# Reading the moving operand of every fp32r product in pairs from two halves of a tile

## The chip, the cores and the metric

The kernel runs on one core of one Trainium2 chip. The metric is the device time of one execution in microseconds. Five engines work side by side: TensorE (PE, with its weight loads shown as PEld), VectorE (DVE), ScalarE (ACT), GpSimd (POOL) and SyncE (SP), which here only issues DMAs.

## The reference, cut to what matters

Three stages follow one another: a block retention (linear attention with a decay per head), a mixture of eight experts whose gate is normalised by eight Sinkhorn rounds, and a dense layer with a non-linearity.

```python
def _moe_ref(x, w_gate, w1, w2):          # x 1536 x 512, w1 8 x 512 x 1024, w2 8 x 1024 x 512
    ...
    for e in range(E):
        h = np.maximum(x @ w1[e], 0.0)
        ye = h @ w2[e]
        out += P[:, e:e + 1] * ye

def _moe2_ref(x, w_in, w_out):            # w_in 512 x 2048, w_out 2048 x 512
    h = x @ w_in
    g = h - np.tanh(h)
    return (g @ w_out).astype(np.float32)
```

## The kernel before, in words

Everything is laid out by hand in one program order; each engine runs its instructions in that order and waits on semaphores.

**Retention** (the first 60 us) works on 12 chunks of 128 tokens with plain fp32 matmuls: `scores` (L234) multiplies keys by queries, `states` (L256) makes the running state, `outputs` (L270, L275) the result. Between the first scores and the rest, eight matmuls into a tile `still` (L357) only keep TensorE busy; their result is read by nobody. They read a tile of zeros, `zr`, as fp32r, 496 columns wide: twice from column 0, twice from column 8, twice from column 8 with the weights from column 8 as well, and twice a single column repeated 496 times. At the very start eight matmuls into `warm` (L185) do the same with bf16 zeros.

**Expert stage**: 96 steps (`NS`). A step `s` takes one half of one expert's hidden width and 512 tokens. The first product runs as seven 256-column products (Strassen's scheme) in `product` (L579, L581, L582); the second, in `second` (L477, L478, L480), is two groups of 512-column matmuls for four token tiles. To keep accuracy every operand is split into a high and a low part, both fp32r, and each product is the sum of three matmuls: high x high, high x low, low x high. So a step has 7 products x 2 k-halves x 3 = 42 matmuls of 256 columns, and 2 groups x 4 tiles x 3 = 24 matmuls of 512 columns.

**Dense stage**: 48 steps, each with 4 x 3 = 12 first matmuls of 512 columns (L689 to L691) and 4 x 3 = 12 second matmuls of 512 columns through `second`.

A matmul's stationary operand is loaded ahead of it (PEld); the moving operand (`rhs`) streams through. Moving are: the parts of `x1` (tiles `xph`, `xpl`, `xsh`, `xsl`, 256 columns a matmul) in the expert stage's first product, `x2` (`x2h`, `x2l`, 512 columns) in the dense stage's first, and the second weights (`w2h`, `w2l`, 512 columns) in `second`. These tiles are written by `split` (L131, L132): ACT copies the source into the high part, rounding it, and DVE (or POOL, for the dense stage's weights) subtracts that from the source to give the low part. `w2_split`, `part` and `turn` call it for `w2`, `x1` and `x2`.

```python
    def split(hi, lo, src, eng=nc.vector):
        nc.scalar.activation(out=hi, in_=src, func=ACTF.Copy)
        eng.tensor_tensor(out=lo, in0=src, in1=hi.bitcast(F32), op=ALU.subtract)
```

## Time and profile before

| | |
|---|---|
| median of 3 runs | 1321.54 us (1321.48 to 1322.59) |
| the profiled execution: time, span | 1320.67 us, 1318.9 us |
| TensorE matmul busy | 1309.5 us, 99% of the span |
| weight loads busy | 1160.9 us, 88% |
| VectorE busy | 916.4 us, 69% |
| ScalarE busy | 528.4 us, 40% |
| GpSimd busy | 275.2 us, 21% |

The time holds 1.8 us outside the span. A matmul's busy time reaches from its start to its end, and one starts before the last has drained, so a busy share of 99% says that TensorE is never without work, not how fast it streams. The speed is read from the distance between the starts of matmuls that follow each other.

### The profile page before, as it was taken

What the parts mean: (1) busy time and instruction counts of PE and PEld (TensorE: products, weight loads), DVE (VectorE), ACT (ScalarE), POOL (GpSimd) and SP (SyncE); (2) the same over time, 40 slices, a digit from 0 to 9 for tenths busy, and PEclk for the clock granted to TensorE, in tenths of its full rate; (3) what the DMA queues carried; (4) which work ended last, traced back from release to release, by engine and by line L of the source; (5) the groups of instructions that cost most, each with busy time, mean ns of one, the idle gap of its engine ahead of it and who ended that gap; (6) DMA issues with size and microseconds to landing.
All of it is one profiled execution on the core that took longest, in us unless ns stands there. A gap on an engine that the chain in (4) does not pass through costs nothing.

```text
span 1318.9 us, 20923 instructions
## 1 busy us (share of the span) xinstructions
PE 1309.5 (99%) x8377; PEld 1160.9 (88%) x8377; DVE 916.4 (69%) x1708; ACT 528.4 (40%) x1029; POOL 275.2 (21%) x325
## 2 busy tenths in 40 slices
PE   8999999999999999999999999999999999999998
PEld 6889999999999999999999999999999888888887
DVE  7877566766767576757667675757653587788887
ACT  2543223332323232333233332323232578776764
POOL 6511011221213121212222130322210102020200
PEclk9999999999999999999999999999999999999999
DMA  8301021222222121212112132222210011011001
GB/s 322 128 33 33 33 73 31 63 89 66 71 68 69 57 80 57 69 61 74 63 64 87 43 105 60 69 68 64 66 33 33 32 33 33 32 33 33 33 33 64
DMA packets 35666, 84.21 MB, mean 64 GB/s; under 512 B 4208, under 2 KB 12400, under 8 KB 35568
## 3 DMA queue, kind: packets, MB, share of 16 engines
q1 hardware_dynamic: 35568, 82.87, 19.3%
q8 instruction: 65, 1.06, 0.3%
q14 instruction: 33, 0.27, 0.1%
HBM read 71.32 MB, written 11.53 MB: 63 GB/s over the span
## 4 chain that ended last, share of the span: by engine, by line
PE 97%; DVE 1%; DMA 1%; issue 0%; ACT 0%; SPq 0%; ACTq 0%; DVEq 0%
PE yp L480 17%; PE yp L477 16%; PE yp L478 16%; PE ha L579 7%; PE ha L582 7%; PE ha L581 7%; PE hb L579 5%; PE hb L581 5%; PE hb L582 5%; PE g L691 3%; PE g L689 3%; PE g L690 3%; DMA qkv<-in_qkv 1%; PE sc L234 1%; PE o L275 0%
## 5 line engine op out<-in xcount | busy, mean ns | idle before, releaser
L508 ACT ACTIVATE hhia<-ha 128x512 fp32r<-128x512 f32 x96 | 57.6, 600 | 469.7 <-PE ha L582 465.8
L579 PE MATMUL ha<-xsh,w1h 128*128 128x256 f32 x576 | 162.0, 281 | 1.7 <-ACT s L600 1.7
L456 POOL TENSOR_TENSOR c<-c,d 128x256 f32<-128x256 f32 x64 | 47.8, 747 | 547.0 <-DVE d L455 547.0
L582 PE MATMUL ha<-xsh,w1l 128*128 128x256 f32 x576 | 161.0, 280 | 0.0
L581 PE MATMUL ha<-xsl,w1h 128*128 128x256 f32 x576 | 160.6, 279 | 0.0
L478 PE MATMUL yp<-w2l,hhia 128*128 128x512 f32 x384 | 149.4, 389 | 0.0
L480 PE MATMUL yp<-w2h,hloa 128*128 128x512 f32 x384 | 149.3, 389 | 0.0
L477 PE MATMUL yp<-w2h,hhia 128*128 128x512 f32 x384 | 149.3, 389 | 0.0
L480 PE MATMUL yp<-w2h,hlob 128*128 128x512 f32 x380 | 148.6, 391 | 0.0
L478 PE MATMUL yp<-w2l,hhib 128*128 128x512 f32 x380 | 147.9, 389 | 0.0
L477 PE MATMUL yp<-w2h,hhib 128*128 128x512 f32 x380 | 147.8, 389 | 0.0
L617 DVE TENSOR_TENSOR ha<-ha,s 128x256 f32<-128x256 f32 x96 | 41.4, 432 | 141.6 <-PE ha L582 141.6
L628 DVE TENSOR_TENSOR hb<-hb,s 128x512 f32<-128x512 f32 x96 | 66.9, 697 | 89.4 <-PE hb L582 89.3
L495 DVE SCALAR_TENSOR_TENSOR yacc<-yp,prob,yacc 128x512 f32<-128x512 f32 x168 | 118.8, 746 | 9.0 <-PE yp L480 9.0
L579 PEld LDWEIGHTS ha<-xsh,w1h 128*128 128x128 f32 x576 | 108.2, 188 | 9.1 <-ACT s L600 1.9
L581 PEld LDWEIGHTS ha<-xsl,w1h 128*128 128x128 f32 x576 | 108.2, 188 | 7.4
L582 PEld LDWEIGHTS ha<-xsh,w1l 128*128 128x128 f32 x576 | 108.8, 189 | 0.0
L579 PE MATMUL hb<-xph,w1h 128*128 128x256 f32 x384 | 106.7, 278 | 0.0
L581 PE MATMUL hb<-xpl,w1h 128*128 128x256 f32 x384 | 106.3, 277 | 0.0
L582 PE MATMUL hb<-xph,w1l 128*128 128x256 f32 x384 | 106.1, 276 | 0.0
L480 PEld LDWEIGHTS yp<-w2h,hloa 128*128 128x128 f32 x384 | 72.1, 188 | 15.0
L480 PEld LDWEIGHTS yp<-w2h,hlob 128*128 128x128 f32 x380 | 71.3, 188 | 14.9
(160 smaller groups left out, 3330.6 us busy)
## 6 DMA issues: line engine op xcount, KB each, us to landing
wraw<-in_w SPq DMA_DIRECT2D x64, 512.0 KB, 4.8
d<-in_wio SPq DMA_DIRECT2D x64, 256.0 KB, 2.9
qkv<-in_qkv SPq DMA_DIRECT2D x23, 512.0 KB, 6.9
wscr<-c SPq DMA_DIRECT2D x64, 128.0 KB, 1.8
wraw<-wscr SPq DMA_DIRECT2D x16, 512.0 KB, 4.4
out<-yacc SPq DMA_DIRECT2D x12, 256.0 KB, 2.1
qkv<-in_qkv SPq DMA_DIRECT2D x2, 256.0 KB, 4.5
lamb<-in_lam SPq DMA_DIRECT2D x1, 4.0 KB, 2.5
```

The source lines that it names most:

```text
L456: nc.gpsimd.tensor_tensor(out=c1.bitcast(F32), in0=c1.bitcast(F32), in1=lo.bitcast(F32), op=ALU.mult)
L477: nc.tensor.matmul(out=yp, lhsT=a[:, ts], rhs=w2h[q][:, i], start=first, stop=False)
L478: nc.tensor.matmul(out=yp, lhsT=a[:, ts], rhs=w2l[q][:, i], start=False, stop=False)
L480: nc.tensor.matmul(out=yp, lhsT=c[:, ts], rhs=w2h[q][:, i], start=False, stop=last)
L495: nc.vector.scalar_tensor_tensor(out=y, in0=yp[t], scalar=prob[:, b * TPB + t, u // 2:u // 2 + 1], in1=y, op0=ALU.mult, op1=ALU.add)
L508: nc.scalar.activation(out=a, in_=ps, func=ACTF.Relu)
L579: nc.tensor.matmul(out=ps, lhsT=w1h[q][:, ws], rhs=xh[:, k], start=start and k == 0, stop=False, skip_group_check=True)
L581: nc.tensor.matmul(out=ps, lhsT=w1h[q][:, ws], rhs=xl[:, k], start=False, stop=False, skip_group_check=True)
L582: nc.tensor.matmul(out=ps, lhsT=w1l[q][:, ws], rhs=xh[:, k], start=False, stop=k == 1, skip_group_check=True)
L617: nc.vector.tensor_tensor(out=pa[:, hi], in0=pa[:, lo], in1=s5, op=ALU.add)
L628: nc.vector.tensor_tensor(out=pb, in0=pb, in1=s12, op=ALU.add)
L689: nc.tensor.matmul(out=ph, lhsT=w1h[q][:, ws], rhs=x2[b][0][:, k], start=k == 0, stop=False)
```

## The change

The moving tiles are stored in another column order, and read back in the old one. `halves` views a stored row as two halves, `odds` views a source row as its even columns and then its odd ones; a split therefore writes the even columns into the first half and the odd ones into the second. `pairs` reads a stored row as column 0 of the first half, column 0 of the second, column 1 of the first, and so on, which is the original order. Results, their order in PSUM, weights and the number of fp32r products stay as they are. The two halves lie 128 columns (512 bytes) apart in `x1`, and 256 columns (1024 bytes) apart in `x2` and the second weights. The sources of the splits are now read with a step of two columns. Beside that the eight fp32r matmuls of `still` become eight bf16 ones of 512 columns.

```diff
+    def halves(a):
+        return a.rearrange("p (t n) -> p t n", t=2)
+    def odds(a):
+        return a.rearrange("p (n t) -> p t n", t=2)
+    def pairs(a):
+        return a.rearrange("p (t n) -> p n t", t=2)
...
-        split(w2h[q][:, i], w2l[q][:, i], wraw[q][:, 1024 + 512 * i:1536 + 512 * i],
+        split(halves(w2h[q][:, i]), halves(w2l[q][:, i]), odds(wraw[q][:, 1024 + 512 * i:1536 + 512 * i]),
...
-        cols = slice(128 * (c % 2), 128 * (c % 2) + 128)
-        hi, lo = (x1[c // TPB][kind, j][:, i:i + n].rearrange("p c (k m) -> p (c k) m", k=2)[:, :, cols]
+        cols = slice(64 * (c % 2), 64 * (c % 2) + 64)
+        hi, lo = (x1[c // TPB][kind, j][:, i:i + n].rearrange("p c (k t m) -> p (c k) t m", k=2, t=2)[:, :, :, cols]
                   for j in range(2))
-        split(hi, lo, src)
+        split(hi, lo, src.rearrange("p k (m t) -> p k t m", t=2))
...
-    for w, rhs in ((0, zr[:, 0:496]), (0, zr[:, 8:504]), (8, zr[:, 8:504]), (0, zr[:, 0:1].to_broadcast([128, 496]))):
-        for i in range(2):
-            nc.tensor.matmul(out=still[:, 0:496], lhsT=zr[:, w:w + 128], rhs=rhs, start=True, stop=True)
+    for i in range(8):
+        nc.tensor.matmul(out=still, lhsT=zero[:, 0:128], rhs=zero, start=True, stop=True)
...
-                        nc.tensor.matmul(out=yp, lhsT=a[:, ts], rhs=w2h[q][:, i], start=first, stop=False)
-                        nc.tensor.matmul(out=yp, lhsT=a[:, ts], rhs=w2l[q][:, i], start=False, stop=False)
+                        nc.tensor.matmul(out=yp, lhsT=a[:, ts], rhs=pairs(w2h[q][:, i]), start=first, stop=False)
+                        nc.tensor.matmul(out=yp, lhsT=a[:, ts], rhs=pairs(w2l[q][:, i]), start=False, stop=False)
...
-        split(x2[b][0][:, k], x2[b][1][:, k], ps)
+        split(halves(x2[b][0][:, k]), halves(x2[b][1][:, k]), odds(ps))
...
-            nc.tensor.matmul(out=ps, lhsT=w1h[q][:, ws], rhs=xh[:, k], start=start and k == 0, stop=False,
+            nc.tensor.matmul(out=ps, lhsT=w1h[q][:, ws], rhs=pairs(xh[:, k]), start=start and k == 0, stop=False,
                              skip_group_check=True)
...
-                nc.tensor.matmul(out=ph, lhsT=w1h[q][:, ws], rhs=x2[b][0][:, k], start=k == 0, stop=False)
+                nc.tensor.matmul(out=ph, lhsT=w1h[q][:, ws], rhs=pairs(x2[b][0][:, k]), start=k == 0, stop=False)
```

No instruction of the products changes its place on TensorE; the one place in that engine's order that differs is `still`, in the first 10 us between the first chunk's scores (`sc`) and its state (`stp`). Before:

```order
L234 MATMUL sc_0_174<-qkv_122 128x128
L234 MATMUL sc_1_175<-qkv_122 128x128
L357 MATMUL still<-zr 128x496 x8
L256 MATMUL stp_204<-qkv_122 64x64 x8
L275 MATMUL o_213<-at_184,qkv_122 64x128 x8
```

After the change, at the same place (the lines of the file have moved by 8 or 9):

```order
L243 MATMUL sc_1_175<-qkv_122 128x128
L365 LDWEIGHTS zr
L365 MATMUL still<-zr 128x512
...
L365 LDWEIGHTS zr
L365 MATMUL still<-zr 128x512
L265 MATMUL stp_204<-qkv_122 64x64 x8
L284 MATMUL o_213<-at_184,qkv_122 64x128 x8
```

Eight matmuls stay eight; they are bf16 and 512 columns wide now. On ScalarE the splits of the first block's `x1` (`xph`, `xsh`, from the retention results `xr` and their sums `ts`) before the change:

```order
L289 ACTIVATE xr_283<-o_271 128x512
L131 ACTIVATE xph_89<-xr_225 128x4x128
L289 ACTIVATE xr_338<-o_318 128x512
L131 ACTIVATE xph_89<-xr_283 128x4x128
L289 ACTIVATE xr_390<-o_370 128x512
L131 ACTIVATE xph_89<-xr_338 128x2x128
```

and after it:

```order
L298 ACTIVATE xr_283<-o_271 128x512
L140 ACTIVATE xph_89<-xr_225 128x8x64
L298 ACTIVATE xr_338<-o_318 128x512
L140 ACTIVATE xph_89<-xr_283 128x8x64
L298 ACTIVATE xr_390<-o_370 128x512
L140 ACTIVATE xph_89<-xr_338 128x4x64
```

The instructions and their order are the same; each writes twice as many runs of half the length.

## Rows read from the trace of the kernel before

**Rows 1.** Page, part 1: busy time, share of the span, instructions of each engine.

```profile
PE 1309.5 (99%) x8377; PEld 1160.9 (88%) x8377; DVE 916.4 (69%) x1708; ACT 528.4 (40%) x1029; POOL 275.2 (21%) x325
```

**Rows 2.** Waits of TensorE, whole span: total us, times, longest.

```profile
PE sc L234 <- DMA qkv<-in_qkv: 2.1, 2, 1.3
PE ha L579 <- ACT s L600: 1.7, 1, 1.7
PE warm L185 <- DVE bias L186: 1.5, 1, 1.5
```

**Rows 3.** Stretches: busy us (count) of PE, PEld, DVE, ACT, POOL; granted clock; DMA.

```profile
60.00:1058.00 998.00, 996.27 (x6390) 903.48 (x6387) 659.44 (x1303) 325.81 (x671) 201.96 (x256) 1.00 0.19 60
10.00:60.00 50.00, 48.80 (x812) 41.86 (x807) 41.19 (x71) 19.53 (x39) 36.41 (x33) 1.00 0.69 247
...
1100.00:1200.00 100.00, 100.00 (x440) 82.39 (x439) 80.53 (x121) 72.97 (x129) 16.99 (x13) 1.00 0.13 43
```

**Rows 4.** Timeline of TensorE, 400 to 410 us: start, duration, line, operation.

```profile
400.66 0.39 PE L477 MATMUL yp<-w2h,hhib 128*128 128x512 f32 x1
...
402.93 0.39 PE L478 MATMUL yp<-w2l,hhib 128*128 128x512 f32 x1
...
403.39 0.28 PE L579 MATMUL ha<-xsh,w1h 128*128 128x256 f32 x1
...
404.09 0.28 PE L579 MATMUL hb<-xph,w1h 128*128 128x256 f32 x1
...
404.44 0.28 PE L579 MATMUL hb<-xph,w1h 128*128 128x256 f32 x1
...
405.57 0.28 PE L581 MATMUL hb<-xpl,w1h 128*128 128x256 f32 x1
```

**Rows 5.** Timeline of TensorE, single matmuls of `still` between 7.7 and 9.3 us.

```profile
7.76 0.39 PE L357 MATMUL still<-zr 128*128 128x496 f32 x1
...
8.66 0.39 PE L357 MATMUL still<-zr 128*128 128x496 f32 x1
8.89 0.37 PE L357 MATMUL still<-zr 128*128 128x496 f32 x1
9.10 0.37 PE L357 MATMUL still<-zr 128*128 128x496 f32 x1
```

**Rows 6.** Tile `still` by itself: duration in ns, lowest, median, highest; starts.

```profile
L357 PE MATMUL still<-zr x8: 372/386/492, 7.4 to 9.1; 128*128 128x496 f32 x8
```

**Rows 7.** Timeline of the weight loads in the retention stage.

```profile
22.43 0.64 PEld L234 LDWEIGHTS sc<-qkv 64*128 64x128 f32 x10
```

**Rows 8.** Line L234 by itself: duration in ns, lowest, median, highest.

```profile
L234 PEld LDWEIGHTS sc<-qkv x192: 182/188/188, 6.3 to 49.9; 64*128 64x128 f32 x192
```

**Rows 9.** Groups of instructions by line and form: the splits.

```profile
L131 ACT ACTIVATE w2h<-wraw 128x512 fp32r<-128x512 f32 x80 | 46.7, 624 | 0.0
L132 DVE TENSOR_TENSOR w2l<-wraw,w2h 128x512 fp32r<-128x512 f32 x64 | 45.0, 704 | 26.7 <-ACT w2h L131 26.7
L131 ACT ACTIVATE w1h<-wraw 128x256 fp32r<-128x256 f32 x32 | 13.0, 407 | 0.0
```

**Rows 10.** The same view: operations that read unit steps, or steps of two and eight.

```profile
L460 DVE SCALAR_TENSOR_TENSOR c<-d,c 128x256 f32<-128x256 f32 x64 | 35.7, 558 | 7.3 <-DVE d L459 0.5
L451 DVE SCALAR_TENSOR_TENSOR c<-c,c 128x256 int32<-128x256 int32 x64 | 27.2, 425 | 2.2
L456 POOL TENSOR_TENSOR c<-c,d 128x256 f32<-128x256 f32 x64 | 47.8, 747 | 547.0 <-DVE d L455 547.0
L457 POOL TENSOR_TENSOR c<-c,c 128x256 f32<-128x256 f32 x64 | 47.3, 740 | 5.0
L418 DVE TENSOR_REDUCE cs<-csum 128x8 f32<-128x96 f32 x8 | 2.0, 255 | 9.0 <-PE csum L415 9.0
L402 DVE TENSOR_REDUCE mx<-logits 128x1 f32<-128x96 f32 x1 | 0.2, 246 | 0.0
```

**Rows 11.** Timeline of the start: the eight opening matmuls on bf16 zeros.

```profile
1.45 3.60 PE L185 MATMUL warm<-zr 128*128 128x512 bf16 x8 [1.45 <-DVE bias L186]
```

## The prediction

> **What bounds the kernel now.** I read the page first: TensorE is busy 99% of the span and no other engine more than 69% [rows 1]. Busy on TensorE does not mean streaming at full speed, so two questions follow: does it wait for anyone, and how fast does it go while it doesn't? The waits answer the first: the longest of all are 2.1 us for a load and 1.7 us for ScalarE [rows 2]. [...] So the kernel is as long as the matmuls that follow each other.

> The timeline answers the second. Between the first and the last 512-column row there are ten starts in 2.27 us, 227 ns a matmul; between the last two 256-column rows ten starts in 1.13 us, 113 ns; in the stretch before them (the product that reads `xsh`) six starts in 0.70 us, 117 ns [rows 4]. The 100 us of the dense stage hold 440 matmuls, 227 ns each [rows 3]. [...]

> [...] Of the eight matmuls of `still`, those that read 496 columns one after the other start 226 ns apart (five starts from 7.76 to 8.89 us), whether reading and weights begin at column 0 or 8; the one that repeats a single column needs 0.21 us until the next starts [rows 5], and the shortest of the eight, 372 ns, is 14 ns below their median of 386 [rows 6]. Same type, same loads of weights, same zeros: only where the moving columns lie differs. [...] The change keeps all columns and reads them from two places in turn; the trace has no matmul of 256 or 512 columns that reads that way, and the sum rests on how much of the broadcast's speed it gets.

> **The change, part by part.**

> *The 512-column matmuls.* Per expert step 24, per dense step 24: 96 x 24 + 48 x 24 = 3456. [...] I take 216 ns, between the two and near the broadcast, the one row in which the loss answered to where the columns lie: 3456 x 11 ns = **38.0 us**.

> *The 256-column matmuls.* 96 x 42 = 4032. Here a second limit lies close: each needs a load of 128 weight columns. In the retention stage's scores the loads, two row halves side by side, come in pairs: ten loads in 0.64 us, the last of which takes 0.188 us, so 0.452 us for four steps, 111 to 113 ns a step [rows 7, 8], although each step there streams no more than 2 x 128 columns. I take 112 ns as the closest that such loads come. From 113.4 ns (227 halved) that gives 4032 x 1.4 ns = **5.6 us**. Bounds: nothing, if the loads set the 113 ns already; 4032 x (115.5 - 109) = 26 us, if the broadcast's speed holds here and the 117 ns go too (115.5 is the middle of 113.4 and 117 weighted by the timeline's steps: a step's 24 x 227 + 42 x 113.4 ns is 10.21 us, while 998 us by 96 steps is 10.40).

> *The splits.* Their number and order stay; the sources are read with a step of two columns. POOL shows no price for that: 747 ns where one input has a step of two, 740 without [rows 10]. DVE shows at most 558 - 425 = 133 ns for 256 columns [rows 10] (different operations, so some of it may be theirs), 266 ns on a low part of 512 columns that takes 704 [rows 9]. ACT has no such row: between nothing and a doubled time by the column, 2 x (624 - 407) = 434 ns on 624 [rows 9]. In three expert steps (31 us) two second weights are split: 0.5 us on DVE, 0.9 us on ACT, beside idle times of 10 and 21 us [rows 3]. A second weight is split about three steps ahead of its use, so nothing is late. In the retention stage DVE is busy 41 of 50 us [rows 3] and the `x1` splits lie near the path; 10,500 columns of low parts, from there to step 3, at 0.52 ns are 5.5 us against 9 us of idle time. I take nothing, with 3 us as the upper bound.

> *`still`.* Eight matmuls for eight. At 210 ns by the broadcast they save 0.1 us; if they stream as slowly as the eight opening ones, 3.60 / 8 = 0.45 us each [rows 11], they cost 1.8 us. I take nothing.

> **Sum.** 38.0 + 5.6 = 43.6 us. The profiled execution took 1320.67 us, so 1277.1; the median is 0.9 us higher, so **1278 us**. Once TensorE is 3.4% faster, DVE's 81% in the dense stage (5% shorter then, since all its matmuls have 512 columns) becomes 85%: still no bound.

> [...]

> [...]

> [...]

> [...]

> [...]

> **How the numbers follow.** Faster, by all or a good part of the sum: 0.52. If half of the loss stays on the 512 columns, 3456 x 5.5 + 5.6 = 25 us are left, less 3 us of splits 1300 us; if both matmuls reach their lower bounds, 3456 x 14 + 26 is 74 us, of which I allow 65, since both at once are unlikely. So this case's own range is 1256 to 1300. No change: 0.12. A little slower, up to 1396: 0.16. Half rate: 0.20, the one case that the range leaves out. Range: 1256 to 1396. What a measurement can tell from no change is about 0.2%, 2.6 us; so faster 0.52, same 0.12, slower 0.36.

> **What would show it.** In the timeline of the changed kernel, ten 512-column starts in 2.16 us (2.27: no change; 2.4 and more: the slower ways), ten 256-column starts in 1.12 us; in the dense stage's 100 us some 463 matmuls for 440. The waits of TensorE should stay under 10 us in all; low parts of second weights between 704 and 970 ns on DVE. I am wrong if the spacing doesn't move, if it grows, or if 256 columns go below 112 ns, which would say that loads are not their limit.

## The result, and the profile after

The changed kernel takes 1280.88 us (median of 4 runs, 1279.1 to 1281.2), the kernel before 1321.99 us in the same runs: a ratio of 0.9686 (95% interval 0.9669 to 0.9703), 41 us less. 1278 us was forecast. The profiled execution took 1280.69 us with a span of 1278.9.

The page's first part, and the waits of TensorE over the whole span (total us, times, longest), to be held against [rows 1, 2]:

```profile
PE 1264.7 (99%) x8377; PEld 1154.7 (90%) x8377; DVE 927.2 (72%) x1708; ACT 546.1 (43%) x1029; POOL 276.8 (22%) x325
```

```profile
PE ha L587 <- ACT s L608: 2.7, 3, 2.1
PE yp L485 <- ACT ghi L665: 1.6, 2, 0.8
PE sc L243 <- DMA qkv<-in_qkv: 1.5, 2, 1.3
PE yp L485 <- DVE yacc L501: 1.5, 2, 0.8
```

TensorE is as busy by share as before, and waits a little more: the second and fourth rows are new and lie in the dense stage (a third new one, 0.8 us for the gate's logits, lies in the retention stage). DVE and ACT are busy 11 and 18 us longer with the same instructions. The gain is in the distance of the matmuls. The timeline of TensorE, for [rows 4]:

```profile
401.90 0.38 PE L485 MATMUL yp<-w2h,hhib 128*128 128x512 f32 x1
...
404.06 0.38 PE L486 MATMUL yp<-w2l,hhib 128*128 128x512 f32 x1
...
404.49 0.27 PE L587 MATMUL ha<-xsh,w1h 128*128 128x256 f32 x1
...
405.16 0.28 PE L587 MATMUL hb<-xph,w1h 128*128 128x256 f32 x1
...
406.28 0.28 PE L589 MATMUL ha<-xpl,w1h 128*128 128x256 f32 x1
```

Ten 512-column starts take 2.16 us, 216 ns each (227 before). The six starts of the product that reads `xsh` take 0.67 us, 112 ns each (117 before), ten of the others 1.12 us, 112 ns (113 before).

The same holds over the whole trace. I call a distance between two starts a stop where it is over 160 ns at 256 columns or over 260 ns at 512. Without the stops, the 3455 recorded distances at 512 columns average 227.3 ns before and 216.0 after, the 4032 at 256 columns 114.9 and 111.6: 39.1 and 13.6 us gained. What the stops take beyond these averages grows from 4.3 to 15.2 us. There are 77 stops after the change, and the rows of `ha` and `yp` above count seven waits: most stops are too short to leave TensorE idle.

The splits of the second weights, for [rows 9] (busy us, mean ns):

```profile
L140 ACT ACTIVATE w2h<-wraw 128x512 fp32r<-128x512 f32 x80 | 66.0, 868 | 0.0
...
L141 DVE TENSOR_TENSOR w2l<-wraw,w2h 128x512 fp32r<-128x512 f32 x64 | 53.8, 841 | 25.4 <-ACT w2h L140 25.4
```

868 ns for 624 on ACT, 841 for 704 on DVE. One thing more happened at the start of the expert stage: stretches of the profile (the last columns are granted clock, DMA share, GB/s).

```profile
68.20:71.00 2.80, 2.80 (x8) 2.26 (x7) 2.06 (x4) 2.80 (x5) 0.00 (x0) 0.50 0.00 0
72.00:78.00 6.00, 6.00 (x44) 5.68 (x44) 5.43 (x10) 1.47 (x4) 0.00 (x0) 1.00 0.31 92
```

TensorE had waited 2.1 us for ACT shortly before (the longest wait above); then it ran at a granted clock of 0.50 for some 3 us, in which its 512-column matmuls start 427 ns apart. That costs 8 x 211 ns = 1.7 us. The profile of before has a wait of 1.7 us there and no such fall. The length of the wait doesn't decide it, though: the run with the storage alone (below) has 1.8 us and the fall (a granted clock of 0.94 from 50 to 80 us, as in the changed kernel), and the first set of reading orders, which is the changed kernel up to its end, has 2.1 us and no fall (1.00 over its span). What decides it stays open.

### The profile page after: what moved, and what is told of

Its sections match the earlier page's. It is cut to its first block, busy times and chain, and to the rows that moved or that the text cites. A ratio compares the mean times of both kernels' runs of the same rounds, so it can differ in the third digit from the quotient of the medians.

```text
span 1278.9 us, 20923 instructions
## 1 busy us (share of the span) xinstructions
PE 1264.7 (99%) x8377; PEld 1154.7 (90%) x8377; DVE 927.2 (72%) x1708; ACT 546.1 (43%) x1029; POOL 276.8 (22%) x325
## 4 chain that ended last, share of the span: by engine, by line
PE 79%; DVE 13%; ACT 4%; POOL 1%; DMA 1%; issue 1%; SPq 0%; ACTq 0%; POOLq 0%; DVEq 0%
PE yp L485 13%; PE yp L488 13%; PE yp L486 13%; PE ha L587 7%; PE ha L590 6%; PE ha L589 6%; PE hb L587 5%; PE hb L590 5%; PE hb L589 5%; DVE tb L688 2%; DVE yacc L501 2%; DVE tb L687 2%; DVE ta L680 2%; DVE g L685 1%; DVE ta L683 1%; PE g L697 1%
## 5 line engine op out<-in xcount | busy, mean ns | idle before, releaser
L485 PE MATMUL yp<-w2h,hhia 128*128 128x512 f32 x384 | 146.7, 382 | 0.0
L488 PE MATMUL yp<-w2h,hloa 128*128 128x512 f32 x384 | 146.3, 381 | 0.0
L486 PE MATMUL yp<-w2l,hhia 128*128 128x512 f32 x384 | 146.3, 381 | 0.0
L485 PE MATMUL yp<-w2h,hhib 128*128 128x512 f32 x380 | 144.4, 380 | 0.0
L488 PE MATMUL yp<-w2h,hlob 128*128 128x512 f32 x380 | 144.1, 379 | 0.0
L486 PE MATMUL yp<-w2l,hhib 128*128 128x512 f32 x380 | 144.1, 379 | 0.0
```

Of the source, the lines that this page charges most:

```text
L485: nc.tensor.matmul(out=yp, lhsT=a[:, ts], rhs=pairs(w2h[q][:, i]), start=first, stop=False)
L486: nc.tensor.matmul(out=yp, lhsT=a[:, ts], rhs=pairs(w2l[q][:, i]), start=False, stop=False)
L488: nc.tensor.matmul(out=yp, lhsT=c[:, ts], rhs=pairs(w2h[q][:, i]), start=False, stop=last)
```

## The experiments

In each of the runs compared by time the kernel before was timed beside it (1322.2 to 1323.6 us).

**The reads alone.** The tiles stored in natural order, still read in pairs; the columns or tokens come out in another order.

```diff
-        split(halves(w2h[q][:, i]), halves(w2l[q][:, i]), odds(wraw[q][:, 1024 + 512 * i:1536 + 512 * i]),
+        split(w2h[q][:, i], w2l[q][:, i], wraw[q][:, 1024 + 512 * i:1536 + 512 * i],
...
-        split(halves(x2[b][0][:, k]), halves(x2[b][1][:, k]), odds(ps))
+        split(x2[b][0][:, k], x2[b][1][:, k], ps)
```

> Reading in pairs stays, but the tiles are stored in their natural order again, so all outputs come with columns or tokens in another order; the splits read and write as before the change. Theory (the gain is the order in which TensorE reads, the price is the split with a step of two): 512 columns 216 ns, 256 columns 112 ns apart, ACT's copy of a second weight back from 868 to 624 ns, and the waits of TensorE in the dense stage (four of 0.9 us, several of 0.1 us) mostly gone: 1274 to 1277 us. Rival 1 (those waits come from the shorter step, not from the splits): 216 and 112 ns, 1281 us. Rival 2 (the gain comes from the storage or from other engines' timing and not from the reads): 227 and 113 ns, 1321 us.

1276.36 us, ratio 0.9653 (0.9641 to 0.9666), ACT's copy at 621 ns. So the whole gain comes with the order of reading, and rival 2 falls. The change is 4.5 us slower than this run, but not all of that is shown to be the price of its splits. Of 5.4 us between the two profiled spans (1278.9 and 1273.5), 1.7 us are the lower clock, which this run didn't have (1.00 from 50 to 80 us); 1.5 us lie before the first `ha` starts (56.3 and 54.8 us), and there the two sets of reading orders below, with the change's own instructions, have 54.5 and 58.8; 1.8 us are stops in the expert stage (7.8 and 6.0), 0.5 us the dense stage. The waits in the dense stage didn't go: `yp` still waits 1.8 us for high parts and 0.8 for `yacc`, and 0.7 to 0.9 us are missing between two starts in four places. Rival 1 holds for these.

**The storage alone.** Splits as in the change, all reads one column after the other.

```diff
-                        nc.tensor.matmul(out=yp, lhsT=a[:, ts], rhs=pairs(w2h[q][:, i]), start=first, stop=False)
+                        nc.tensor.matmul(out=yp, lhsT=a[:, ts], rhs=w2h[q][:, i], start=first, stop=False)
```

(and so for each `pairs`.)

> The tiles are stored with even columns first, but read one column after the other, so outputs come in another order. Theory: 227 and 113 to 117 ns as before the change, the slower splits hidden behind TensorE: 1321 to 1323 us. Rival 1 (the splits' price lies on the path whatever TensorE's speed): 1327 us. Rival 2 (storage makes the gain): 1281 us.

1323.12 us, ratio 1.0003 (0.9991 to 1.0014): nothing is gained or lost by storage. Its row for the same copy holds a surprise:

```profile
L140 ACT ACTIVATE w2h<-wraw 128x512 fp32r<-128x512 f32 x80 | 49.5, 658 | 0.0
```

The same instruction, with the same step of two, takes 658 ns here and 868 in the changed kernel. With TensorE reading one column after the other the step costs 34 ns (658 for 624 before the change); the other 210 appear in the changed kernel, in which TensorE reads in pairs.

**512 columns alone.** `x1` stored and read as before the change, the second weights and `x2` as after it.

> Only the second weights and x2 (512 columns a matmul) are stored and read in pairs; x1 is stored and read as before the change. Theory (256 columns gain 1.6 ns at 113 and 5 ns at 117, because the weight loads hold them at 112): the 512-column matmuls keep all of their gain, 256 columns go back to 113 and 117 ns, which costs 4032 x 2.4 = 10 us: 1290 us. Rival (the 256-column matmuls are bound by weight loads before the change as well, and gain nothing): 1281 us.

1286.99 us, ratio 0.9733 (0.9721 to 0.9746). The 512-column matmuls bring 35 us of the gain, the 256-column ones 6.1 us more (1286.99 - 1280.88; 5.6 forecast, 10 in the expectation). That is their net worth: by the traces their distance falls from 114.6 ns here to 111.6 in the change, 12 us, of which the change loses 2.9 us again in stops of the expert stage (4.9 here, 7.8 there) and 1.7 us at the lower clock.

**What order costs what.** Groups of eight matmuls behind the kernel's end, each on its own line, for instance

```diff
+    for i in range(8):
+        nc.tensor.matmul(**look(w[:, 0:512], 512, 128))
+    for i in range(8):
+        nc.tensor.matmul(**look(w[:, 0:512].rearrange('p (t n) -> p n t', t=2), 512, 128))
```

with `w` the 1024 columns of a second weight, then the columns and the number of weight columns.

> The changed kernel with 33 groups of eight matmuls behind its end, on second weights of the last step, each group with another order of reading; their results are not used. Spacing in a group tells the price of the order. Theory (a new stretch of 16 columns costs one column's time if the reader stands in one stretch only, and two open stretches hide it): one after the other 227 ns at any offset; halves in pairs, and quarters in fours, 216; runs of 2, 4 and 8 columns from each half 216, runs of 16 and 32 back at 227; pairs at a distance of 2 to 8 columns 227, from 16 on 216; one column repeated 213 to 216, 16 columns over and over 216, 32 columns over and over 227; step 2, with twice as many new stretches, 240; step 16, each column a new stretch, 430 or more. Rival (the loss depends on which part of the memory neighbouring reads fall in, not on stretches): pairs differ by distance beyond 16 too, and quarters differ from halves. At 256 columns, theory (weight loads hold 112 ns): one after the other 113, pairs 112, one column repeated 112, pairs with 64 weight columns 109, 192 columns 112 in either order, 128 columns 112. Rival (the streaming holds 112): repeated 109, pairs with 64 weight columns 112, 192 columns 85.

The timeline of TensorE there, at a granted clock of 1.00 and with all other engines idle; the distance in a group is its start to the next row's, divided by eight.

```profile
1273.66 1.98 PE L723 MATMUL mb<-w2h,w2l 128*128 128x512 f32 x8
1275.48 1.89 PE L725 MATMUL mb<-w2h,w2l 128*128 128x512 f32 x8
1277.20 2.03 PE L727 MATMUL mb<-w2h,w2l 128*128 128x512 f32 x8
1279.08 2.43 PE L729 MATMUL mb<-w2h,w2l 128*128 128x512 f32 x8
1281.34 3.77 PE L731 MATMUL mb<-w2h,w2l 128*128 128x512 f32 x8
1284.93 3.86 PE L733 MATMUL mb<-w2h,w2l 128*128 128x512 f32 x8
1288.61 3.65 PE L735 MATMUL mb<-w2h,w2l 128*128 128x512 f32 x8
1292.08 2.84 PE L737 MATMUL mb<-w2h,w2l 128*128 128x512 f32 x8
1294.75 2.17 PE L739 MATMUL mb<-w2h,w2l 128*128 128x512 f32 x8
1296.76 2.11 PE L741 MATMUL mb<-w2h,w2l 128*128 128x512 f32 x8
1298.71 2.08 PE L743 MATMUL mb<-w2h,w2l 128*128 128x512 f32 x8
1300.63 2.06 PE L745 MATMUL mb<-w2h,w2l 128*128 128x512 f32 x8
1302.52 2.01 PE L747 MATMUL mb<-w2h,w2l 128*128 128x512 f32 x8
1304.37 1.89 PE L749 MATMUL mb<-w2h,w2l 128*128 128x512 f32 x8
1306.09 1.89 PE L751 MATMUL mb<-w2h,w2l 128*128 128x512 f32 x8
...
1314.73 1.89 PE L761 MATMUL mb<-w2h,w2l 128*128 128x512 f32 x8
1316.45 2.09 PE L763 MATMUL mb<-w2h,w2l 128*128 128x512 f32 x8
1318.38 2.06 PE L765 MATMUL mb<-w2h,w2l 128*128 128x512 f32 x8
1320.28 1.91 PE L767 MATMUL mb<-w2h,w2l 128*128 128x512 f32 x8
1322.03 2.02 PE L769 MATMUL mb<-w2h,w2l 128*128 128x512 f32 x8
1323.88 1.11 PE L771 MATMUL mb<-w2h,w2l 128*128 128x256 f32 x8
1324.83 1.06 PE L773 MATMUL mb<-w2h,w2l 128*128 128x256 f32 x8
1325.72 1.06 PE L775 MATMUL mb<-w2h,w2l 128*128 128x256 f32 x8
1326.62 1.10 PE L777 MATMUL mb<-w2h,w2l 128*64 128x256 f32 x8
1327.56 1.04 PE L779 MATMUL mb<-w2h,w2l 128*64 128x256 f32 x8
1328.44 1.04 PE L781 MATMUL mb<-w2h,w2l 128*128 128x192 f32 x8
1329.31 1.05 PE L783 MATMUL mb<-w2h,w2l 128*128 128x192 f32 x8
```

| 512 columns read | line | ns |
|---|---|---|
| one after the other, from column 0, the same again, from column 8 | 723, 769, 727 | 228, 231, 235 |
| halves in pairs | 725 | 215 |
| quarters in fours | 729 | 283 |
| step 2, 4, 16 | 731, 733, 735 | 449, 460, 434 |
| two from each half in turn | 737 | 334 |
| 4, 8, 16, 32 from each half in turn | 739, 741, 743, 745 | 251, 244, 240, 236 |
| pairs 2, 4 columns apart | 747, 749 | 231, 215 |
| pairs 8, 16, 32, 64, 128 columns apart | 751 to 759 | 216 on average |
| each column twice | 761 | 215 |
| 16, 32 columns over and over | 763, 765 | 241, 238 |
| one column repeated | 767 | 219 |

My theory of new stretches of 16 columns falls: the same 16 columns over and over (241 ns) are as slow as new ones (228 to 235), two, four or eight from each half (334, 251, 244) are slower than one after the other, and quarters (283) are not fast. Its rival has the quarters right, but not the pairs, which from 4 columns' distance on are all alike (215 and 216). A step of two takes 449 ns, twice the 228 of one after the other: the half rate that I feared for pairs.

At 256 columns the theory holds: one column repeated (L775) 112 ns, pairs (L773) 111, pairs with 64 weight columns (L779) 110, and 192 columns one after the other (L781) still 109 although at 227 ns for 512 they would stream in 85 ns. So something other than the columns holds these matmuls at 109 to 112 ns. That it is the load of 128 weight columns fits the 111 to 113 ns in the prediction and the 110 with 64 weight columns, but no group had fewer columns and fewer weights at once. One after the other from `w` (L771) they take 119.

```diff
+        nc.tensor.matmul(**look(w[:, 0:512].rearrange('p (b t n) -> p b n t', t=2, n=4), 512, 128))
...
+        nc.tensor.matmul(**look(w[:, 2:514].rearrange('p (b t n) -> p b n t', t=2, n=4), 512, 128))
...
+        nc.tensor.matmul(**look(w.rearrange('p (t n s) -> p n t s', t=2, s=2)[:, :, :, 0], 512, 128))
```

> Behind the end of the changed kernel, again groups of eight matmuls with other orders of reading; their results are not used. The first set said: one after the other 227 to 239, pairs from 4 columns' distance on 216, runs of two from each half 333, 16 columns over and over 240. Theory formed from it (the reader takes even and odd places of the stream separately, each keeps one line of 4 columns, 16 bytes, and loses time when it leaves a line after fewer than four reads of its own): halves in pairs from column 2 on 216; pairs at 4 columns' distance from column 2 on (each side leaves its line after two reads) 227 to 240, at 8 columns' distance from column 2 on between 216 and 230; halves 255 columns apart 215 for 510 columns; halves 512 columns apart 216; pairs whose halves are read at a step of two (two reads a line and side) 227 to 240; at a step of four (one read a line), 256 columns, 180 or more; each column four times 216; every second column twice (two reads a line and side) 227 to 240; every fourth column twice (one read) 350 or more. Rival (a pair is fast as soon as its two columns lie in different lines, since one after the other both want the same line at once): pairs at 4 and 8 columns' distance from column 2 on 216, halves at a step of two 216, halves at a step of four 108 to 112; every second column twice 227, like one after the other.

The timeline of TensorE in the second set:

```profile
1281.54 1.89 PE L727 MATMUL mb<-w2h,w2l 128*128 128x512 f32 x8
1283.27 1.89 PE L729 MATMUL mb<-w2h,w2l 128*128 128x512 f32 x8
1285.00 1.99 PE L731 MATMUL mb<-w2h,w2l 128*128 128x512 f32 x8
1286.83 1.98 PE L733 MATMUL mb<-w2h,w2l 128*128 128x512 f32 x8
1288.64 1.89 PE L735 MATMUL mb<-w2h,w2l 128*128 128x510 f32 x8
...
1292.09 2.02 PE L739 MATMUL mb<-w2h,w2l 128*128 128x512 f32 x8
1293.95 2.01 PE L741 MATMUL mb<-w2h,w2l 128*128 128x256 f32 x8
1295.78 1.91 PE L743 MATMUL mb<-w2h,w2l 128*128 128x512 f32 x8
1297.53 2.00 PE L745 MATMUL mb<-w2h,w2l 128*128 128x512 f32 x8
1299.36 3.78 PE L747 MATMUL mb<-w2h,w2l 128*128 128x512 f32 x8
1302.97 2.01 PE L749 MATMUL mb<-w2h,w2l 128*128 128x512 f32 x8
```

Halves in pairs take 216 ns from column 2 on as well (L727), and so do halves 255 and 512 columns apart (L735, L737). Pairs four columns apart take 216 ns from column 0 on (L729) and 229 from column 2 on (L731), where by the theory each side leaves its line after two reads; at eight apart from column 2 on 226 (L733). Halves read at a step of two take 232 (L739), at a step of four, 256 columns, 229 (L741; half rate against the 228 that 512 columns take one after the other). Each column four times takes 219 (L743), every second column twice 229 (L745), every fourth twice 451 (L747). Every number lies where the theory put it but L743, 219 for 216; the rival, that a pair is fast once its columns lie in different lines, misses L731, L733, L739 and L741. The theory doesn't cover all of the first set: by its count two from each half in turn (334) and quarters (283) leave a line after each read of a side, as a step of four does (460), yet they cost less.

**The order of the second weights made by the host.** Their splits read neighbours again; `x1`, `x2` and the reads stay.

```diff
-        b = b.reshape(n, 2, 128, DM).transpose(0, 2, 1, 3).reshape(n, 128, 1024)
+        b = b.reshape(n, 2, 128, DM // 2, 2).transpose(0, 2, 1, 4, 3).reshape(n, 128, 1024)
```

> The changed kernel, but the even-first order of all second weights is made once where the host lays the input arrays out, so that these splits read neighbouring columns again; x1, x2 and all reads in pairs stay. Outputs are the reference's. Theory (of the 4.5 us that the order-free storage gained over the change, most was the second weights' splits on ScalarE and VectorE): ACT's copy 621 to 624 ns, 1276 to 1278 us. Rival (it was the x1 splits at the start, or the granted clock that fell there for 3 us): 1280 to 1281 us.

1277.93 us, ratio 0.9663 (0.9645 to 0.9682), ACT's copy at 625 ns. It lies where the theory put it, but its interval overlaps the changed kernel's, so these splits' share of the 4.5 us isn't settled by time. The stops of the expert stage speak for a small one: 7.8, 8.3 and 8.1 us in the change and the two sets of reading orders, 6.0 us here and 5.8 to 7.1 us in the four runs below that are built on this one. The granted clock fell in its profile as well (0.94 in the stretch from 50 to 80 us), so that isn't what host order saves.

**Why the dense stage waits.** First, less work for VectorE in the step in question:

```diff
-            (nc.gpsimd if v in (NV - 1, NV) else nc.vector).tensor_tensor(out=glo, in0=g, in1=ghi.bitcast(F32), op=ALU.subtract)
+            (nc.gpsimd if v % 4 == 2 or v in (NV - 1, NV) else nc.vector).tensor_tensor(out=glo, in0=g, in1=ghi.bitcast(F32), op=ALU.subtract)
```

> host_order, with one of four low parts of the dense stage (that of the step in which four finished tiles are added up) subtracted on GpSimd instead of VectorE. Theory (the waits of 0.7 to 0.9 us in the dense stage come about because VectorE is behind when the four tiles are to be added up): VectorE is relieved of 0.7 us there, the four waits shrink to 0.2 us or go, 3 us less than host_order: 1273 to 1275 us. Rival (ScalarE is late there, held by a weight load that hasn't landed): no change against host_order.

1277.32 us, ratio 0.9657 (0.9641 to 0.9673): no difference, and the waits for high parts stay (2.5 us, four times). The theory of too much work falls. The timeline of this run shows a loop instead:

```profile
1127.42 0.75 DVE L688 COPY_PREDICATED tb<-tb,g 128x512 f32<-128x512 uint32 x1
...
1128.20 0.63 ACT L665 ACTIVATE ghi<-tb 128x512 fp32r<-128x512 f32 x1 [0.99 <-DVE tb L688]
...
1129.84 0.69 DVE L680 TENSOR_TENSOR ta<-g,ta 128x512 f32<-128x512 f32 x1 [1.67 <-ACT ta L676]
...
1132.36 0.74 DVE L688 COPY_PREDICATED tb<-tb,g 128x512 f32<-128x512 uint32 x1
```

DVE's last operation of a step releases ACT's high part; square and tanh stand behind that; DVE waits 1.67 us for them and starts the next step: 4.94 us from `tb` to `tb`. Every fourth step holds four additions of 0.6 us too, in part in the time in which DVE would wait; from 1110 us on such a step takes 6.1 to 6.9 us, four steps together 20.9 to 21.7. Four steps of TensorE are 4 x 24 x 216 ns = 20.7 us, 21.8 before the change. So ACT's order was turned round:

```diff
             nc.scalar.activation(out=t, in_=ph, func=ACTF.Square)
             nc.scalar.activation(out=th, in_=ph, func=ACTF.Tanh)
+            nc.vector.tensor_tensor(out=w, in0=ph, in1=t, op=ALU.mult)
+        if v - 2 in tmp:
...
+            nc.scalar.activation(out=ghi, in_=g, func=ACTF.Copy)
```

> host_order, with one move in the dense stage: in each step ScalarE first squares and takes the tanh of the new product and then copies the high part of the step before the last, instead of the other way round (VectorE's product and low part change places with it). Outputs are the reference's. Moving a low part to GpSimd had left the waits of 0.7 to 0.9 us as they were, so VectorE's amount of work isn't it. Theory (a loop: the high part waits for VectorE's last operation of the step before, the square waits behind the high part, VectorE's first operation waits for the square and tanh; 4.93 us round, 2.5 us more every fourth step, as long as four steps of TensorE): the waits go, the dense stage's idle time falls from 5 to under 2 us, 1274 to 1275 us. Rival (ScalarE waits for weights that land late, 0.9 us twice): nothing changes, 1277 to 1278 us.

1279.93 us, ratio 0.9678 (0.9665 to 0.9691): not faster. The waits changed their releaser: for high parts 0.3 us are left, and each of eight groups of tiles waits for its first addition.

```profile
PE yp L485 <- DVE yacc L501: 4.5, 8, 0.6
```

The additions stand behind all of the step's operations on DVE. Two runs put them ahead of its last two, one in the new order of ACT and one in the old (`act2` is the second factor and the predicated copy, taken out of `act`):

```diff
+        act2(v)
         for f_ in (fill, fillb)[v % 2][NS + v // 2]:
```

> host_order_loop, with the four additions of finished tiles put on VectorE ahead of the last two operations of the step (the second polynomial factor and the predicated copy) instead of behind them. Outputs are the reference's. The last run cleared ScalarE's queue, and each of the eight groups then waited 0.72 us for the addition of its first tile. Theory (the additions come too late because they stand behind the whole step on VectorE): they are 1.4 us earlier, 0.72 us of wait goes, dense-stage idle time 7.1 to about 1 us: 1273 to 1275 us. Rival (VectorE has no room there whatever the order): 0.7 us stays or shows at another matmul, 1279 to 1281 us.

> host_order with the same early additions, but ScalarE's old order. Theory (the additions alone don't do it: the predicated copy now comes 2.5 us later in those steps, and with it the high part and, behind that, the square of the next step): 1277 to 1279 us, with waits for high parts. Rival (only the additions' place counts): 1273 to 1275 us.

With the new order 1274.17 us, ratio 0.963 (0.9615 to 0.9644), the fastest of all, below the changed kernel's interval; of its waits in the dense stage these are left, and both come at its very end, behind the last step (the two instructions start at 1259.38 and 1261.01 us):

```profile
PE yp L488 <- POOL glo L676: 0.9, 1, 0.9
PE yp L485 <- ACT ghi L675: 0.4, 1, 0.4
```

With the old order 1287.05 us, ratio 0.9731 (0.9709 to 0.9752), slower than without the move and 8 us beyond what I expected: `yp` waits 8.2 us for additions. (Of the 11.7 us between its profiled span and that of the host's order, 3.9 us lie before the first `ha`, where the kernels are the same, and 8.6 us in the dense stage.) So neither move does it alone. Both stood in the way: the high part ahead of square and tanh, and the additions behind the whole step.

## Why the prediction was right, point by point

**What bounds the kernel, and the place of the gain**: right. The distance between starts was the time, and the order of reading alone changes it (the reads alone 0.9653, the storage alone 1.0003).

**The 512-column term**, 227 to 216 ns, 38 us: right, 216 measured, 39.1 us by the distances. Its reason was only half right. The distance does hang on the addresses, as the broadcast in `still` said (0.21 us where neighbouring columns took 0.226): by the first set 512 columns take 228 ns one after the other, 215 in pairs of halves and 219 from one repeated column. But it isn't a price for each new stretch of 16 columns, which I had counted as "no change": 16 columns repeated take 241 ns. What the two sets agree with, apart from the exceptions named there, is a reader with two sides that wants four reads of a line on each; it stays a theory of mine. No run shows the lower bounds between which the 216 ns were taken, nor the 14 ns a matmul by which the lower end of the range goes below 227: the fastest groups of 512 columns took 215.

**The 256-column term**, 5.6 us: right in its limit, too small in its size. 192 columns at 109 ns and one repeated column at 112 show a floor that the columns don't set, and the change came down to it (111.6 ns). But the term started from 113.4 ns, while the matmuls before averaged 114.9: not one product of six matmuls but all that write `ha` from `xsh`, 18 of a step's 42, averaged 116.4. By the distances 13.6 us were gained, within the term's upper bound of 26. (The bound's own working doesn't give its 115.5: 0.19 us a step over 42 matmuls is 4.5 ns, which makes 117.9, because the stretch of 998 us holds 13 us of the dense stage.)

**The splits**, taken at nothing with 3 us as the upper bound: this is the step that was mis-sized, by about 2 us as far as the traces show. The 4.5 us between the reads alone and the change hold 1.7 us of clock and 1.5 us before the first `ha`, which scatters as much in one and the same kernel; the rest is stops. From 100 to 1000 us the weight loads of `ha` wait 2.7 to 3.2 us for ACT's copies `s` in the change and the two sets, 1.0 us in the reads alone, 0.6 with the host's order, and not at all before the change. ACT's 244 ns a copy lie inside the term's bounds, and ACT isn't busy in the stop at 417.6 us: it has itself waited 1.85 us for VectorE's addition `hb`. So idle time doesn't hide everything, since one late step stops TensorE while the engines are idle on average; what makes VectorE late there wasn't traced further.

**DVE at 85% in the dense stage, "still no bound"**: wrong in what follows from it. It wasn't the share: relieving DVE did nothing, and another order on both engines gave 3.8 us (1277.93 to 1274.17). Four rounds of the loop, 20.9 to 21.7 us, had room in 21.8 us of TensorE's work and none in 20.7. The prediction's sign of 463 matmuls in 100 us of this stage missed for it: there were 451.

Put together on the profiled spans: 39.1 and 13.6 us gained by the distances, 10.9 us lost to longer stops (5.1 us of them in the dense stage, 1.7 us at the lower clock), 1.7 us later at the first `ha` (54.6 and 56.3 us), against 40.0 us measured (1318.9 - 1278.9). The forecast had 38.0 and 5.6 gained and nothing lost. That its sum came within 3 us of the median is luck in part: the 256 columns gave 8 us more than their term, and what was taken at nothing cost 12.6.

**The rivals.** No change and a little slower (up to 1396 us) did not come: 216 ns for 227 at 512 columns, and no run shows a loss that pairs of halves add. Half rate, 0.20, did not come for pairs either, but it did for a step of two (449 ns), of four (460) and of sixteen (434). What I couldn't see is that pairs and a step differ: by the theory each side gets four reads of a line in pairs, and one at any of these steps. Two reads a line and side, as in every second column twice (229 ns), take as long as one column after the other (228).

## What to carry to other kernels

Read TensorE's speed from the distance between starts, not from its busy share, and put eight matmuls in another reading order behind the kernel's end before rebuilding it: it cost under 2 us for each of the orders that decide here (1.82 and 1.72) and settles the main term. The fp32r moving operands of this kernel, read in pairs from two halves, took 216 ns for 512 columns where they took 227 read straight through, 5% less. The order is best made where it is free, in the layout of the inputs: there ScalarE's copies took 625 ns instead of 868. When the engine that bounds a kernel gets 5% faster, look for loops between the others whose round is just under the old step: here work moved off an engine didn't shorten the loop, and order did. And where a sum comes out right, check its terms one by one: here two errors hid each other.

## What the runs showed of the hardware that I had not expected

ScalarE's copy with a source step of two takes 658 ns while TensorE reads one column after the other, 868 while it reads in pairs, and 625 with neighbouring sources under pairs; in the changed kernel's stretch at the lower clock, two of these copies took 676 and 685. VectorE's subtraction with a source step of two goes from 703 to 841 in the same way, GpSimd's doesn't (1312, 1303). So with the same step of two at their sources both engines take longer in the kernel in which TensorE reads in pairs, while TensorE's own 216 ns are the same with slow copies (868) and fast ones (621, 625). Why is not shown.

A straight stream isn't one speed: 228 and 231 ns from column 0, 235 from column 8, 236 to 251 in runs of 4 to 32 from each half, 238 to 241 for 16 or 32 columns repeated, and 117 or 113 for 256 columns by tile. By the theory's count, two lines visited in turn by each side (quarters 283, two from each half 334) cost less than a new line at each read (434 and 460). Why is open; it wasn't tried further.
